# Attention and feed-forward on one core: the first batch's queries and keys in two transfers, and a given order of decoding, mix and scores

## The chip, the cores and the metric

The kernel runs on one core of one Trainium2 chip. A core has five engines with instruction streams of their own: TensorE (PE; its weight loads are listed apart as PEld), VectorE (DVE), ScalarE (ACT), GpSimd (POOL) and SyncE (SP), whose queue issues the transfers between device memory and the on-chip memory. The metric is the device time of one execution in microseconds (us); less is better.

## The reference

The inputs are 8 batches of 8 heads with 512 local and 32 global tokens of 64 numbers. A local query attends to the 32 global keys and to the local keys at most 32 positions away; a global query attends to all 544 keys. The result, as 576 tokens of 512 numbers, goes through a feed-forward part that mixes each token with the one ahead of it:

```python
    s_g = scale * np.matmul(q_g, k_all.transpose(0, 1, 3, 2))
    out_g = np.matmul(sm(s_g), v_all)
    mask = np.abs(pos[:, None] - pos[None, :]) <= window
    s_ll = np.where(mask, s_ll, -1000000000.0)
    a_l = sm(np.concatenate([s_lg, s_ll], axis=-1))
    out_l = np.matmul(a_l, np.concatenate([v_g, v_l], axis=2))
...
    xk = mu_k * x + (1.0 - mu_k) * x_prev
    xr = mu_r * x + (1.0 - mu_r) * x_prev
    k = np.maximum(xk @ w_k, 0.0)
    v = k * k @ w_v
    r = 1.0 / (1.0 + np.exp(-(xr @ w_r)))
    return (r * v).astype(np.float32)
```

The queries, keys and values are float32 and the weights w_k (512 x 1024), w_r (512 x 512) and w_v (1024 x 512) are float64.

## The kernel before, in words

**Attention.** Two heads lie side by side on the 128 partitions as one unit, so that a batch has four units, and two units make a pair. For each unit one array `qk` holds on 128 rows the 64 columns of global queries, the 512 of local queries and the 896 of windows of keys (1536 columns, 768 KB), and another, `v`, the values. `scores` (the multiplications are recorded at L359 in `Run.matmul`) multiplies queries of 64 tokens with a window of 160 keys on PE. DVE adds the mask and takes the greatest of each row (L331), ACT takes exponentials and their sums (L337, eight for a call), DVE makes the inverse of the sums (L294, L295) and POOL multiplies by it (L347, four operations, into `Pt` and `Pgl`). `scores_global` does the like for the global queries of a pair (L411 and L415 on DVE, L419 on ACT, L421 on POOL, result `Pg`). `transposes` and `transposes_of_g` turn the result on PE (L384, L393), and DVE and ACT copy it to `PT` and `PTg` (L386, L394); `transposes_global` does this for `Pg` (L434, copies to `PG` at L435). `weighted` multiplies by the values and copies the tokens to `xT` (L488 on ACT) and to `xg_all` (L483 and L485 on DVE).

**Batch 0.** Its two pairs are cut into halves of 256 tokens. This gives four groups of scores, here R0 (pair 0, first half), R1 (pair 1, first half), R2 (pair 0, second half) and R3 (pair 1, second half), and two global ones. From batch 1 on a generator interleaves the attention of the next batch with the feed-forward part of the one before.

**Feed-forward.** `Tokens` stands for 256 tokens. `Tokens.mix` computes for two blocks of 128 numbers at a time (`c0` is 0 or 2) the difference to the token ahead (L521) and, for the keys (`xk`) and then the gate (`xr`), the mixed value `xfull` (L525). ACT rounds it to a first part (L529: `xkh`, `xrh`), and POOL makes the rest (L530: `xkl`, `xrl`). Block 0 comes from pair 0 and block 2 from pair 1. `keys_and_gate` makes `xk @ w_k` with three products for each pair of blocks (L496, L497, L498, in `products`: first part by first part of the weight, rest by first part, first part by rest), then `relu` on ACT (L541), its square on POOL (L543) and as first part and rest on ACT (L546) and DVE (L547). `gates` and `values` do the same with w_r and w_v.

**Weights.** The float64 weights are read as 64-bit integers in 20 chunks of 128 x 512 (512 KB): 0 to 7 of w_k, 8 to 11 of w_r, 12 to 19 of w_v. `decode` makes float32 of them: ACT scales the high word (L192), DVE shifts and joins the bits in three operations (L193, L196, L199), ACT rounds to a first part (L205) and POOL subtracts (L206), so that `wk_h` and `wk_l` (or `wr`, `wv`) sum to the weight. The first four chunks have a buffer each. The others share a ring of three: the load of chunk n+3 (`load_chunk`, L177) waits for POOL's L206 of chunk n. `weights` is a generator; each `next(decoding)` decodes one chunk and asks for the next load.

**Order.** Each engine runs its instructions in one fixed order. The tile scheduler makes it at build time, from the program's order of statements, a model of times and explicit constraints: `tc.issue_after(i)` keeps what is recorded within it behind instruction `i`. Transfers are issued by SP in the order in which the loads are written (L282 for `raw_qk`, L287 for `raw_v`, L177 for chunks, L854 for `mu_k` and `mu_r`). The start of batch 0 is written out by hand at the end of the main function. Eight masks, one for each half and each of four places, are made by POOL with 16 `affine_select` (L126, L130).

## Time and profile before

| what | value |
|---|---|
| median of three runs | 693.78 us (692.35, 693.78, 924.29) |
| the profiled execution | 695.92 us |
| its span, from first to last instruction | 694.0 us |
| mean granted clock of TensorE | 0.98 |
| moved by DMA | 123.37 MB, 178 GB/s over the span |
| queue issues of `w_k` chunks, median to landing | 9.7 us |
| queue issues of `w_r` chunks, median to landing | 4.0 us |

The run of 924.29 us is far from the two others and is left out of every reading. The profiled execution is one more execution; it spends 1.9 us outside its span. In a timeline a row gives the start, the duration, the engine, line and operation, output and inputs, and in brackets the idle time ahead of it with what ended it. Line numbers are those of the kernel before.

### The profile page before, as it was taken

To read this page: it belongs to the slowest core of one execution; us is meant where nothing else is said; L and a number is where in the kernel's file an instruction comes from. 1 tells how busy PE (TensorE), PEld (TensorE's weight loads), DVE (VectorE), ACT (ScalarE), POOL (GpSimd) and SP (SyncE) were. 2 spreads that over 40 slices of the span, in tenths; PEclk is the share of its full clock that TensorE was granted. 3 is DMA by queue.
4 is the path that set the end of the run, shared out by engine and by line. 5 is a ranking of instruction groups with operands and counts; after the bars stand their busy time and mean duration, and the time that the engine had idled before them with its cause. 6 is when DMAs were issued, how large, how long until landed. Compare 5 with 4: busy or idle time off the path is not lost.

```text
span 694.0 us, 18613 instructions
## 1 busy us (share of the span) xinstructions
PE 659.8 (95%) x7472; PEld 621.6 (90%) x7472; DVE 428.0 (62%) x1217; ACT 387.0 (56%) x1058; POOL 360.1 (52%) x363
## 2 busy tenths in 40 slices
PE   4879999999998899999999999999999999999997
PEld 2658788999897899999999999999999999999996
DVE  5767987356647575555685656646675656377531
ACT  5756886356355456566557473757366644453530
POOL 5656596137967434564428353655348342642810
PEclk9659999999999999999999999999999999999999
DMA  9732535153736641452909083644728081535666
GB/s 343 295 97 104 212 124 196 47 184 122 245 137 239 213 175 75 157 209 105 350 7 338 26 318 138 221 145 180 277 76 291 2 323 43 197 119 170 204 198 207
DMA packets 43542, 123.37 MB, mean 178 GB/s; under 512 B 4032, under 2 KB 20928, under 8 KB 43456
## 3 DMA queue, kind: packets, MB, share of 16 engines
q1 hardware_dynamic: 43456, 122.18, 49.4%
q8 instruction: 59, 0.97, 0.6%
q14 instruction: 27, 0.22, 0.1%
HBM read 104.86 MB, written 17.30 MB: 176 GB/s over the span
## 4 chain that ended last, share of the span: by engine, by line
PE 63%; DVE 12%; POOL 9%; DMA 8%; ACT 5%; issue 3%; SPq 0%; POOLq 0%; ACTq 0%; DVEq 0%
PE ps_m L652 14%; PE ps_m L497 11%; PE ps_m L496 11%; PE ps_m L498 11%; PE ps_s L363 8%; DMA a<-scratch 6%; PE ps_t L384 3%; ACT Pt L337 2%; DVE xfull L525 2%; DVE diff L521 2%; DMA w<-w_r 2%; DVE Pt L331 2%; PE ps_s L365 1%; POOL Pt L347 1%; DVE kkl L547 1%
## 5 line engine op out<-in xcount | busy, mean ns | idle before, releaser
L496 PE MATMUL ps_m<-xkh,wk_h 128*128 128x256 f32 x544 | 154.9, 285 | 2.2 <-ACT xkh L529 1.0
L497 PE MATMUL ps_m<-xkl,wk_h 128*128 128x256 f32 x544 | 153.5, 282 | 0.5 <-POOL xkl L530 0.4
L498 PE MATMUL ps_m<-xkh,wk_l 128*128 128x256 f32 x544 | 153.2, 282 | 0.0
L652 PE MATMUL ps_m<-bh,a 128*128 128x256 f32 x736 | 137.8, 282 | 2.8 <-DMA a<-scratch 2.8
L337 ACT ACTIVATE Pt<-Pt,m 128x160 f32<-128x160 f32 x256 | 106.5, 418 | 29.0 <-DVE m L331 27.7
L652 PEld LDWEIGHTS ps_m<-bh,a 128*128 128x128 f32 x736 | 115.0, 188 | 6.1 <-DMA a<-scratch 3.1
L347 POOL TENSOR_TENSOR Pt<-Pt,ssum 128x512 f32<-128x512 f32 x64 | 67.9, 1061 | 82.2 <-DVE ssum L295 34.9
L496 PEld LDWEIGHTS ps_m<-xkh,wk_h 128*128 128x128 f32 x544 | 103.1, 190 | 4.1 <-ACT xkh L529 1.2
L497 PEld LDWEIGHTS ps_m<-xkl,wk_h 128*128 128x128 f32 x544 | 103.0, 189 | 1.6 <-POOL xkl L530 1.0
L498 PEld LDWEIGHTS ps_m<-xkh,wk_l 128*128 128x128 f32 x544 | 103.0, 189 | 0.3 <-issue 0.2
L652 PE MATMUL ps_m<-bl,a 128*128 128x256 f32 x368 | 102.6, 279 | 0.0
L530 POOL TENSOR_TENSOR xkl<-xfull,xkh 128x512 fp32r<-128x512 f32 x34 | 46.7, 1374 | 89.8 <-ACT xkh L529 84.8
L564 DVE TENSOR_TENSOR B<-ps_m,relu 128x512 f32<-128x512 f32 x52 | 35.9, 690 | 72.3 <-ACT relu L562 72.3
L562 ACT ACTIVATE relu<-ps_m 128x512 f32<-128x512 f32 x52 | 31.1, 597 | 83.8 <-PE ps_m L498 81.6
L496 PE MATMUL ps_m<-xrh,wr_h 128*128 128x256 f32 x272 | 77.2, 284 | 0.4 <-ACT relu L541 0.4
L497 PE MATMUL ps_m<-xrl,wr_h 128*128 128x256 f32 x272 | 76.3, 281 | 0.0
L498 PE MATMUL ps_m<-xrh,wr_l 128*128 128x256 f32 x272 | 76.1, 280 | 0.0
L331 DVE CUSTOM_DVE_ANT_0 Pt<-ps_s,masks 128x160 f32<-128x160 f32 x256 | 65.6, 317 | 7.4 <-PE ps_s L363 7.3
L652 PEld LDWEIGHTS ps_m<-bl,a 128*128 128x128 f32 x368 | 69.2, 188 | 0.0
L599 POOL TENSOR_TENSOR gate<-sum,gate 128x512 f32<-128x512 f32 x18 | 26.9, 1493 | 58.9 <-DVE sum L698 39.2
L205 ACT CAST bh<-B 128x512 fp32r<-128x512 f32 x76 | 45.9, 619 | 17.3 <-PE ps_m L652 10.8
L496 PEld LDWEIGHTS ps_m<-xrh,wr_h 128*128 128x128 f32 x272 | 51.5, 189 | 1.1 <-ACT relu L541 0.5
(138 smaller groups left out, 1586.1 us busy)
## 6 DMA issues: line engine op xcount, KB each, us to landing
a<-scratch SPq DMA_DIRECT2D x92, 512.0 KB, 6.2
raw_qk<-qk SPq DMA_DIRECT2D x32, 768.0 KB, 5.7
raw_v<-v SPq DMA_DIRECT2D x32, 640.0 KB, 6.4
out_l<-gate SPq DMA_DIRECT2D x32, 256.0 KB, 4.8
w<-w_k SPq DMA_DIRECT2D x8, 512.0 KB, 9.7
w<-w_v SPq DMA_DIRECT2D x8, 512.0 KB, 4.2
w<-w_r SPq DMA_DIRECT2D x4, 512.0 KB, 4.0
scratch<-wv_h SPq DMA_DIRECT2D x8, 256.0 KB, 2.7
```

Source lines behind the costliest of these rows:

```text
L205: nc.scalar.copy(hi, val)
L331: read = nc.vector.tensor_tensor_reduce(out=Pt[:, i], in0=place(e, t, h), in1=masks[:, e, slots[t][1]], op0=ALU.add, op1=ALU.min, scale=-s ...
L337: nc.scalar.activation(Pt[:, i], Pt[:, i], AF.Exp, bias=low_x[:, i:i + 1], scale=-1.0, accum_out=ssum[:, i:i + 1],)
L347: nc.gpsimd.tensor_mul(out, Pt[:, each, at:at + n], rinv.unsqueeze(2).to_broadcast([P, 4, n]))
L363: self.last = nc.tensor.matmul(*a, **kw)
L496: nc.tensor.matmul(out, w_h[:, i, cols], x_h(i), start=(i == 0), stop=False)
L497: nc.tensor.matmul(out, w_h[:, i, cols], x_l(i), start=False, stop=False)
L498: nc.tensor.matmul(out, w_l[:, i, cols], x_h(i), start=False, stop=(i == n - 1))
L530: nc.gpsimd.tensor_sub(lo[:, both], xf, hi[:, both].bitcast(F32))
L562: nc.scalar.activation(rk, kp, AF.Relu)
L564: nc.vector.tensor_mul(k2[f0 // HC][f0 % HC // 2], kp, rk)
L652: nc.tensor.matmul(out[:, j], w, x[:, i % 2], start=fresh and (i, j, n) == (0, 0, 0), stop=(i, n) == (HC - 1, 2), skip_group_check=True,)
```

## The change

It has five parts, all in the start of batch 0.

1. The columns of `qk` are put as global queries, first 256 local queries, keys, last 256 local queries. For batch 0 a unit is loaded in two transfers, of 832 columns (these hold the global queries, the first local queries and the keys of the first half) and of 704. The four first parts are issued ahead of everything else; the chunks come behind the second parts and values. For other batches it is one transfer as before, and `q(i)` finds a block of queries in the new order.
2. Four of the eight masks, which are equal to others, are copied by DVE, and the 16 selects become 8.
3. `mix` takes which mix to make (`of`) and for which blocks (`c0s`). For the first 256 tokens of batch 0 the mix for the keys of block 0, then of block 2, then the mix for the gate are recorded apart, and for the second 256 tokens the keys and the gate apart. The difference (L521) is computed in each call, so there are eight more of them in all.
4. `queued_after` puts what is recorded in it behind given instructions. With it, chunk 0 stands behind the copies of R0's transposes, chunk 1 behind those of R1, chunks 2 and 3 behind the first mix for the keys, R2's scores behind the second one and the values of the first halves, and chunks 4 and 5 and R3's scores behind the mix for the gate. Chunks 2 and 3 use the four-bank pool of PSUM instead of the two-bank one.
5. `weighted` returns its last matmul and copy, so that these can be waited for.

```diff
+    @contextmanager
+    def queued_after(*before):
+
+        with ExitStack() as stack:
+            for i in before:
+                stack.enter_context(tc.issue_after(i.ins))
+            yield
...
     def load_qk(s, pool=rawp, tag=""):
-        s.qk = pool.tile([P, K0 + SK], F32, tag="qk" + tag, name="raw_qk")
-        nc.sync.dma_start(out=s.qk, in_=qk[s.b, s.c])
-        s.q, s.k = s.qk[:, QG:K0], s.qk[:, K0:]
+
+        if s.b > 0:
+            cols = slice(None)
+        elif s.qk is None:
+            cols = slice(FIRST_PART)
+        else:
+            cols = slice(FIRST_PART, None)
+        if s.qk is None:
+            s.qk = pool.tile([P, QG + SL + SK], F32, tag="qk" + tag, name="raw_qk")
+            s.k = s.qk[:, K0:K0 + SK]
+        nc.sync.dma_start(out=s.qk[:, cols], in_=qk[s.b, s.c][:, cols])
...
-    load_qk(heads_0[0])
+    load_first(load_qk, range(NC))
+    load_first(load_qk, (0, 1))
+    load_first(load_v, (0, 1))
     load_chunk()
-    load_qk(heads_0[1])
+    load_first(load_qk, (2, 3))
     load_chunk()
...
     for sb, mu in ((mu_k_sb, mu_k), (mu_r_sb, mu_r)):
         nc.sync.dma_start(out=sb, in_=mu)
-    for _ in range(3):
+    load_first(load_v, (2, 3))
+    for _ in range(5):
         load_chunk()
-    R, Pg = [], []
-    for pair, bank in zip(pairs_0, "os"):
-        R.append(by_halves(pair, 0))
-        Pg.append(scores_global(pair, bank))
+    R = [by_halves(pair, 0) for pair in pairs_0]
+    Pg = scores_global(pairs_0[0], "o")
+    with queued_after(all_transposes(R[0])):
+        next_Pg = scores_global(pairs_0[1], "s")
+    with queued_after(*R[0].copies[1:]):
         next(decoding)
-    for i, pair in enumerate(pairs_0):
-        all_transposes(R[i])
-        PG, final, _ = transposes_global(Pg[i])
-        with tc.issue_after(final.ins):
-            weighted(pair, xTs_0[i], PG, (0,), "m")
+    PG, final, _ = transposes_global(Pg)
+    all_transposes(R[1])
+    with queued_after(*R[1].copies[1:]):
         next(decoding)
-        if i == 0:
-            R.append(by_halves(pair, 1))
+    with queued_after(final):
+        weighted(pairs_0[0], xTs_0[0], PG, (0,), "m")
+    PG, final, _ = transposes_global(next_Pg)
+    first[0].mix("k", (0,))
+    with queued_after(*first[0].mix_ends):
+        for _ in range(2):
+            next(decoding)
+    with queued_after(final):
+        values_made, _ = weighted(pairs_0[1], xTs_0[1], PG, (0,), "m")
+    first[0].mix("k", (2,))
+    with queued_after(values_made, *first[0].mix_ends):
+        R.append(by_halves(pairs_0[0], 1))
+    first[0].mix("r")
...
-    first[0].mix()
     next(keys[0])
     next(keys[0])
-    next(decoding)
-    next(decoding)
-    R.append(by_halves(pairs_0[1], 1))
+    with queued_after(*first[0].mix_ends):
+        next(decoding)
+        next(decoding)
+    with queued_after(values_made, *first[0].mix_ends):
+        R.append(by_halves(pairs_0[1], 1))
...
+        first[1].mix("k")
         for _ in keys[0]:
             next(decoding)
             yield
-        first[1].mix()
+        first[1].mix("r")
```

The lines of the changed kernel have other numbers: L282 becomes L313 (`raw_qk`), L287 L317 (`raw_v`), L177 L186 (chunks), L192 L201 (scaling), L205 and L206 L214 and L215 (rounding and split), L488 L518 (`xT`), L435 L465 (`PG`), L529 and L530 L563 and L564, L347 L377, L543 L581.

The loads on SP at the very start, before:

```order
L282 DMA raw_qk<-qk 128x1536
L177 DMA w_190<-w_k 128x512
L282 DMA raw_qk<-qk 128x1536
L177 DMA w_194<-w_k 128x512
L282 DMA raw_qk<-qk 128x1536 x2
L287 DMA raw_v<-v 128x1280 x2
L177 DMA w_204<-w_k 128x512
L177 DMA w_206<-w_k 128x512
L287 DMA raw_v<-v 128x1280 x2
```

and of the change:

```order
L313 DMA raw_qk<-qk 128x832 x4
L313 DMA raw_qk<-qk 128x704 x2
L317 DMA raw_v<-v 128x1280 x2
L186 DMA w_182<-w_k 128x512
L313 DMA raw_qk<-qk 128x704 x2
L186 DMA w_186<-w_k 128x512
```

The first chunk was the second transfer; it now stands behind eight others. (The names with `w_` are chunks; each number is one buffer.)

ACT around the copies of the first tokens (`xT`), before:

```order
L192 ACTIVATE w_216<-w_216 128x512
L192 ACTIVATE w_218<-w_218 128x512
L488 COPY xT<-ps_t 128x2x2x64
L205 CAST wk_h<-w_204 128x512
L205 CAST wk_h<-w_214 128x512
L205 CAST wk_h<-w_216 128x512
L488 COPY xT<-ps_t 128x2x2x64
L386 COPY PT<-ps_t 128x512
L529 CAST xkh<-xfull 128x512
```

and of the change:

```order
L201 ACTIVATE w_186<-w_186 128x512
L518 COPY xT<-ps_t 128x2x2x64
L201 ACTIVATE w_202<-w_202 128x512
L214 CAST wk_h<-w_186 128x512
L518 COPY xT<-ps_t 128x2x2x64
L465 COPY PG<-ps_t 128x512
L465 COPY PG<-ps_t 128x128
L563 CAST xkh<-xfull 128x512
```

The scaling of `w_202`, chunk 6 and the last that is issued at the start, now stands between the two copies of the first pair's tokens, and the first `xkh` follows the copies of `PG`.

POOL's splits of the chunks of w_k and the first of w_r, from the first `xkl` on, before:

```order
L530 TENSOR_TENSOR xkl<-xfull,xkh 128x512
L530 TENSOR_TENSOR xrl<-xfull,xrh 128x512
L206 TENSOR_TENSOR wk_l<-w_218,wk_h 128x512
...
L206 TENSOR_TENSOR wk_l<-w_290,wk_h 128x512
L206 TENSOR_TENSOR wk_l<-w_206,wk_h 128x512
L530 TENSOR_TENSOR xkl<-xfull,xkh 128x512
L530 TENSOR_TENSOR xrl<-xfull,xrh 128x512
L543 TENSOR_TENSOR k_643<-relu 128x512
L543 TENSOR_TENSOR k_676<-relu 128x512
L206 TENSOR_TENSOR wr_l<-w_362,wr_h 128x512
```

and of the change, from the second `xkl` on:

```order
L564 TENSOR_TENSOR xkl<-xfull,xkh 128x512
...
L564 TENSOR_TENSOR xrl<-xfull,xrh 128x512 x2
L581 TENSOR_TENSOR k_633<-relu 128x512
L215 TENSOR_TENSOR wk_l<-w_198,wk_h 128x512
L581 TENSOR_TENSOR k_666<-relu 128x512
L215 TENSOR_TENSOR wk_l<-w_200,wk_h 128x512
...
L215 TENSOR_TENSOR wk_l<-w_202,wk_h 128x512
L215 TENSOR_TENSOR wk_l<-w_355,wk_h 128x512
...
L215 TENSOR_TENSOR wr_l<-w_392,wr_h 128x512
```

In each place that is left out stand the four norms of one group of scores (L347, now L377). The splits of chunks 4 to 7 (`w_198`, `w_200`, `w_202`, `w_355`) stood ahead of the second `xkl` and now stand behind it, behind the first squares and between norms.

More of the change, by code (lines that the diff above doesn't have):

```diff
@@ L1 @@
-from contextlib import ExitStack
+from contextlib import ExitStack, contextmanager
 from itertools import chain
@@ L119, in local_global_attention_then_rwkv_ffn, with in_window @@
     nc.gpsimd.memset(masks, 0.0)
[L120 to L133 removed]
+    def in_window(e, p, a):
+        return masks[a * BL:(a + 1) * BL, e, p, SG * e:SG * e + W]
+    same = {}
+    for e, p in ((1, 0), (0, 0), (0, 1), (1, 1)):
+        for a, i in enumerate(PAIRS[e][p]):
+            m = in_window(e, p, a)
+            ahead = FIRST[i] - BL * i + SG
+            if (a, ahead) in same:
+                nc.vector.tensor_copy(m, same[a, ahead])
+                continue
+            same[a, ahead] = m
+            nc.gpsimd.affine_select(
+                out=m, in_=m, pattern=[[1, W]], base=ahead, channel_multiplier=-1,
+                compare_op=ALU.is_ge, fill=NEG,
+            )
+            nc.gpsimd.affine_select(
+                out=m, in_=m, pattern=[[-1, W]], base=2 * SG - ahead, channel_multiplier=1,
+                compare_op=ALU.is_ge, fill=NEG,
+            )
     low = const.tile([P, 3 * W], BF16, name="low")
@@ L491, in weighted @@
                 )
+        return run.last, copied
     def products(out, w_h, w_l, cols, x_h, x_l, n):
@@ L510, in wide, with mix @@
             return mixp.tile([P, NC, TOK], dtype, tag="mix", name=name)
-        def mix(self):
+        def mix(self, of="kr", c0s=range(0, NC, 2)):
             got = []
-            for mu, nm in ((mu_k_sb, "k"), (mu_r_sb, "r")):
-                got.append((mu, self.wide(f"x{nm}h", F32R), self.wide(f"x{nm}l", F32R)))
-            for c0 in range(0, NC, 2):
+            for x in of:
+                if x not in self.mixed:
+                    self.mixed[x] = tuple(self.wide(f"x{x}{part}", F32R) for part in "hl")
+                got.append(({"k": mu_k_sb, "r": mu_r_sb}[x], *self.mixed[x]))
+            for c0 in c0s:
                 both = slice(c0, c0 + 2)
@@ L528, in mix @@
                         )
-                    nc.scalar.copy(hi[:, both], xf)
+                    cut = nc.scalar.copy(hi[:, both], xf)
                     nc.gpsimd.tensor_sub(lo[:, both], xf, hi[:, both].bitcast(F32))
-            (_, self.xk_h, self.xk_l), (_, self.xr_h, self.xr_l) = got
+                    if x == "k":
+                        self.xk_h, self.xk_l = hi, lo
+                    else:
+                        self.xr_h, self.xr_l = hi, lo
+            self.mix_ends = mixed, cut
         def keys_and_gate(self):
@@ L830, in local_global_attention_then_rwkv_ffn @@
     keys = [t.keys_and_gate() for t in first]
-    decoding = weights(range(EARLY), wk_h, wk_l, "m")
+    decoding = chain(weights(range(2), wk_h, wk_l, "m"), weights(range(2, EARLY), wk_h, wk_l))
     def by_halves(pair, p):
```

45 lines of the change are left out of this document (17 added, 28 removed).

## The prediction

> **What bounds the kernel now.** I read the page first, then the busy time by stretches, then the timelines of the engines around the places that the diff touches. The page says whose kernel it is:
>
> ```profile
> span 694.0 us, 18613 instructions
> PE 659.8 (95%) x7472; PEld 621.6 (90%) x7472; DVE 428.0 (62%) x1217; ACT 387.0 (56%) x1058; POOL 360.1 (52%) x363
> ```
>
> PE is busy 95% of the span, so only the 34.2 us in which it is not can be won, besides time in which it works slowly. The stretches (busy us of PE, PEld, DVE, ACT, POOL; then the granted clock and the DMA share) say where both lie:
>
> ```profile
> 0.00:56.00 56.00, 37.86 (x397) 27.19 (x397) 38.16 (x139) 34.24 (x105) 33.00 (x55) 0.76 0.63 235
> 56.00:112.80 56.80, 54.41 (x625) 48.73 (x626) 48.85 (x137) 45.24 (x126) 39.90 (x38) 1.00 0.49 169
> 112.80:117.80 5.00, 4.20 (x39) 3.96 (x37) 2.80 (x4) 2.93 (x8) 5.00 (x7) 1.00 0.50 203
> 117.80:694.00 576.20, 563.32 (x6416) 541.73 (x6416) 338.17 (x938) 304.62 (x821) 282.17 (x266) 1.00 0.49 173
> ```
>
> The first 56 us hold 18.1 us of idle PE and a clock of 0.76; the 576 us behind 117.8 hold 12.9 us of idle PE. The change touches the first part alone: from the values of batch 0 on, PE's instructions stand in the same order before and after, and so, in kind, do those of the other engines. So the whole effect is how much earlier or later PE passes one place, the product with the last piece of w_v, which ends the start:
>
> ```profile
> 4.93 1.34 PE L359 MATMUL ps_s<-raw_qk 64*64 64x160 f32 x16 [4.93 <-DMA raw_qk<-qk]
> 55.95 0.39 PE L497 MATMUL ps_m<-xkl,wk_h 128*128 128x256 f32 x1 [0.45 <-POOL xkl L530]
> 117.78 0.38 PE L498 MATMUL ps_m<-kkh,wv_l 128*128 128x256 f32 x1 [0.80 <-POOL wv_l L206]
> ```
>
> The three rows (start, duration, what ended the idle time) are the start's three marks: the first keys land at 4.93, the mixed tokens of the second pair reach PE at 55.95, the last decoded weight reaches it at 117.78. Between the second and third mark PE waits little, yet it is not alone: every chunk has to pass through ACT, DVE, ACT and POOL, and the next load into the ring of three waits for POOL:
>
> ```profile
> SPq L177 <- POOL wk_l L206: 23.7, 4, 10.9
> SPq L177 <- POOL wv_l L206: 23.1, 5, 12.1
> SPq L177 <- POOL wr_l L206: 8.1, 3, 4.2
> ```
>
> (Total us, times, longest.) These are waits of the load queue up to 120 us; 12 of the chunks' loads leave only when an older chunk is through. So there are two chains: tokens to PE up to 56, and chunks to PE up to 117.8. An earlier end needs both.
>
> **The change, part by part. The first loads.** Now the first scores wait for transfers and masks thus:
>
> ```profile
> 5.80 1.65 POOL L130 TENSOR_SCALAR_AFFINE_SELECT masks<-masks 64x128 bf16<-64x128 bf16 x5
> 6.78 0.67 ACT L192 ACTIVATE w<-w 128x512 f32<-128x512 f32 x1 [4.76 <-DMA w<-w_k]
> 9.57 0.33 DVE L331 CUSTOM_DVE_ANT_0 Pt<-ps_s,masks 128x160 f32<-128x160 f32 x1
> 10.80 0.41 ACT L337 ACTIVATE Pt<-Pt,m 128x160 f32<-128x160 f32 x1
> 18.90 0.41 ACT L337 ACTIVATE Pt<-Pt,m 128x160 f32<-128x160 f32 x1
> ```
>
> Masks are complete at 7.45, chunk 0 is decoded ahead of the scores on DVE, and the exponentials of the first halves (R0 and R1) end at 19.3. After the change 0.43 MB instead of 0.79 MB must land for a unit. Rates, from the 5-us stretches:
>
> ```profile
> 10.00:15.00 5.00, 2.71 (x37) 1.48 (x35) 4.59 (x23) 5.00 (x20) 1.44 (x2) 0.97 1.02 424
> 25.00:30.00 5.00, 3.82 (x77) 3.50 (x76) 3.73 (x9) 4.92 (x17) 1.70 (x3) 0.83 0.97 394
> 30.00:35.00 5.00, 5.00 (x40) 3.79 (x37) 4.96 (x9) 2.02 (x4) 5.00 (x5) 0.50 0.07 22
> 45.00:50.00 5.00, 5.00 (x59) 4.66 (x58) 1.91 (x7) 1.46 (x3) 4.79 (x6) 0.50 0.33 108
> ```
>
> The last number is GB/s: the transfers fill the DMA engines up to 30 us at some 0.41 MB/us. The part left out is 0.36 MB, 0.85 us, so the first unit lands at 4.93 − 0.85 = 4.1 and each further first part 1.05 later. Eight selects become four copies on DVE; eight times 0.33 (1.65 for five) leaves the masks ready at about 4.8. Scores of R0 then start near 5.8 instead of 9.57, since no decoding stands ahead of them, and 8 exponentials of 0.41 run from 6.2 to 9.5. R1 needs the second pair's parts (8.3 and 9.2 with the load order) and ends its exponentials near 15.5: 3.8 us ahead of 19.3. The four extra transfers cost SP about 0.45 us each at the issue; the queue is behind the DMA engines' rate anyway, so nothing on the path.
>
> **The tokens.** From there I followed the new order by durations of rows: transposes, values of the first pair 21.4 to 24.5 on PE, copy of its tokens by ACT at 23.3. Next in ACT's order stands the scaling of chunk 6, the last of the 9.44 MB issued at the start. At 0.407 MB/us from 3.1 on, that lands at 26.3; so a new wait of 2.6 us on ACT, with the second token copy, two PG copies and the first xkh behind it, and DVE's mix and PE's next values behind those. It is of the kind that this row shows before, where token copies stand behind the scaling of a chunk that lands late:
>
> ```profile
> 50.18 0.69 ACT L192 ACTIVATE w<-w 128x512 f32<-128x512 f32 x1 [2.83 <-DMA w<-w_r]
> 50.77 0.62 ACT L488 COPY xT<-ps_t 128x256 f32<-128x256 f32 x2
> 51.15 0.89 DVE L521 TENSOR_TENSOR diff<-xT 128x256 f32<-128x256 f32 x1 [4.24 <-ACT xT L488]
> 54.61 1.28 POOL L530 TENSOR_TENSOR xkl<-xfull,xkh 128x512 fp32r<-128x512 f32 x1 [2.85 <-ACT xkh L529]
> ```
>
> With it, the first xkh comes at 29.0, the second pair's values at 28.6 to 33.8 (half clock), the second xkh at 37.6 and its xkl at 39.5 in place of 55.9. That is 16.4 us earlier; 1.8 us of PE work which stood ahead of the mark (scores of R3, transposes of R2) now stands behind it, so PE's lead is 14.6 us. The extra differences on DVE, eight with 4 of them here, at this price, and the multiplications of the gate's mix, which no longer stand in the way, are in that chain:
>
> ```profile
> 35.43 0.41 DVE L521 TENSOR_TENSOR diff<-xT 128x256 f32<-128x256 f32 x1
> ```
>
> **The chunks.** At 39.5 only chunks 0 to 3 are decoded; before, the last of eight was split at 51.8:
>
> ```profile
> 49.19 2.57 POOL L206 TENSOR_TENSOR wk_l<-w,wk_h 128x512 fp32r<-128x512 f32 x2
> ```
>
> Chunks 4 and 5 come behind the scores of R2 and the mix for the gate, 6 and 7 behind R3. The marks of the last gate chunk (11) are now:
>
> ```profile
> 64.96 0.39 SPq L177 DMA_DIRECT2D w<-w_r  x1
> 69.66 0.69 ACT L192 ACTIVATE w<-w 128x512 f32<-128x512 f32 x1 [1.59 <-DMA w<-w_r]
> 70.38 0.69 DVE L193 TENSOR_SCALAR ps_s<-w 128x512 int32<-128x512 int32 x1 [1.40 <-ACT w L192]
> 73.38 1.44 POOL L206 TENSOR_TENSOR wr_l<-w,wr_h 128x512 fp32r<-128x512 f32 x1 [1.05 <-ACT wr_h L205]
> 75.64 0.39 PE L498 MATMUL ps_m<-xrh,wr_l 128*128 128x256 f32 x1
> ```
>
> The load leaves at 64.96, DVE is on it at 70.38 and PE uses it at 75.64. A load of this kind takes 4.0 us to landing when it goes alone:
>
> ```profile
> w<-w_r SPq DMA_DIRECT2D x4, 512.0 KB, 4.0
> ```
>
> In the new order, by pitches of 0.6 for an operation of ACT or DVE on 128x512, 0.25 for a score, 0.41 for an exponential, 1.3 for a split and some 3 for four norms: the first relu is at 43.0 and chunk 4 is scaled behind it (43.6), its split ends at 50.4; chunk 7's load leaves then and lands at 54.3. Chunk 5's split at 52.8 frees chunk 8, scaled at 60.0 behind six exponentials of batch 1; chunks 6 and 7 are split by 58.6 and 59.9. Chunk 8's split, behind another pair of norms, ends at 69.0, and chunk 11 loads from 69.0 to 73.0: DVE on it at 73.7, **3.3 us later** than before. PE's 14.6 us are gone in waits for chunks 4 to 11. From chunk 11 on, the rows that carry the rest are
>
> ```profile
> 75.60:113.50 37.90, 35.51 (x408) 31.38 (x404) 34.43 (x109) 31.68 (x90) 26.72 (x26) 1.00 0.53 184
> 99.67 1.79 DVE L547 TENSOR_TENSOR kkl<-k,kkh 128x512 fp32r<-128x512 f32 x1 [0.33 <-POOL k L543]
> 103.34 0.61 DVE L415 CUSTOM_DVE_ANT_0 Pg<-ps_t,low,mg 128x384 f32<-128x384 f32 x1
> 112.08 0.69 DVE L199 SCALAR_TENSOR_TENSOR w<-w,ps_s 128x512 int32<-128x512 int32 x1
> 112.96 1.06 POOL L347 TENSOR_TENSOR Pt<-Pt,ssum 128x512 f32<-128x512 f32 x1
> 115.71 0.58 POOL L347 TENSOR_TENSOR Pgl<-Pt,ssum 128x128 f32<-128x128 f32 x1
> 116.25 1.48 POOL L206 TENSOR_TENSOR wv_l<-w,wv_h 128x512 fp32r<-128x512 f32 x1
> ```
>
> DVE is busy 34.4 of 37.9 us there: its order is the bound, not PE. Between chunk 11 and the last chunk it has in the new order one kkl (1.3 as a mean of such rows), one global score (0.8) and three small copies (0.4) fewer and two differences (0.8) more: **−1.7**. Of its 3.5 idle us I credit **−0.5**, since PE's results now wait for it. On POOL the four norms (112.96 to 116.29) stand between the last two splits; in the new order they stand ahead of both, where they start some 2.5 us before DVE ends. The last split then comes 3.2 us behind DVE's end instead of 5.0: **−1.8**. Sum: 3.3 − 1.7 − 0.5 − 1.8 = −0.7.
>
> A second way to the same end: of DVE's 38.2 us up to 56, the new order has at 39.5 left for later four chunks (12 operations, 7.4), R3's scores (2.0), the gate's mix (1.6) and a transpose copy (0.6), so some 26 to 27 are done. Of 87 us up to the last decoding, plus 3.3 for eight differences, less 1.7 put behind it, 62.5 remain. At the share of the second stretch (48.85 of 56.80, 86%) this ends at 39.5 + 72.7 = 112.2, against 112.77; with POOL's −1.8, −2.4. I take the middle of the two ways, **−1.5**. At the 91% of the row above it would end at 108.3 and the sum be −6.3; without any idle time at 102: these bound the gain, and no case of a gain beyond 12.6 is left unless DVE does less.
>
> **A rule that speaks against it.** PE's waits for chunks 4 to 11 could cost clock. The two 5-us rows above, at 30 and 45, show PE busy for all of 5.00 us at a granted 0.50, and the second stretch shows 1.00. The Trainium skill, page "TensorE: Matmul & The Clock Gate", section "Part 1: The HAM clock gate", says that TensorE falls to half rate after an idle window of about 3.4 us and comes back only after a busy one; by that rule each long wait would cost an estimated 1.7 us behind it. The trace agrees in that rows of both 0.50 and 1.00 exist, but not that a busy stretch suffices. Without the rule: a wait for chunk 11 longer than any PE has now would leave some 5 us at 0.50 as in those rows, a loss of 2.5 us each. As long as it comes ahead of 77, PE waits for chunk 11 anyway and it is hidden; behind that it is not.
>
> **The rivals.** (a) *The decoding keeps up*: chunk 6 lands earlier than 26.3 or the norms of R2 and R3 are cheaper to pass, chunk 11 is not late, DVE runs at 91%. The gain is 4.0 (the sum without its +3.3) to 8; 686 to 690. For it speaks that ACT and POOL have idle time in all stretches; against it, that all five late loads hang on splits queued behind scores and relus. (b) *The chunks set the end, later*: the place is chunk 8's split, which frees chunk 11's load. Each us that it ends after 64.9 goes to the end, since DVE has nothing to catch up with; it decides from 3.5 us on, where the credits on DVE and POOL (4.0) are spent. With DVE's credits gone (+2.2) the sum is +1.5, and with chunk 8 behind four more norms (3.3) it is +4.8: 695 to 699, slower than before. For it: chunk 8 is scaled behind exponentials of the next batch. (c) *The clock*: two waits behind 77 at 2.5 us, 5.0 with the −1.5: about 697. (d) *The lead is kept*: the decoding is not in the way at all, −14.6, 679. DVE's 62.5 us left speak against it. That the first loads do not come earlier can be left out: a first part has 54% of the bytes.
>
> **How the numbers follow.** The forecast has 0.45, (a) 0.26, (b) 0.21, (c) 0.04, (d) 0.04. The profiled execution took 695.9 us (694.0 of it in the span), 2.1 above the median of 693.8. 695.9 − 1.5 = 694.4 for such an execution, **692.3** against the median. Range: down to 685, most of (a), up to 700, nearly all of (b) and (c). Two per cent, what a measurement of this kernel can tell, are 13.9 us: faster by that only with (d) and no trouble, 0.05 with the tail of (a); slower by that 0.03; within it 0.92.
>
> **What would show it.** Right: first score on DVE near 5.8 and exponentials of R1 done by 15.5; the scaling of chunk 6 waiting for its load with token copies behind; the second xkl near 39.5; PE idle by some 12 us or more between 40 and 78, waiting for wk and wr pieces; chunk 11's load leaving at 67 to 71; DVE 85 to 91% busy from 40 on; the last wv_l at 115 to 118. Wrong: PE still 5 us or more ahead at the gate's fourth chunk (before 70.6), which is (a) or (d); the last wv_l behind 119, which is (b) if chunk 11 was late, (c) if the clock shows below 1.00 behind 77.

## The result, and the profile after

The change is slower: 703.25 us as the median of four runs (700.53 to 705.41). Its ratio to the kernel before on the same chip is 1.0107 with a 95% interval of 1.0068 to 1.0146, some 7.4 us. The kernel before has a median of 693.78 us in three runs of that comparison; a fourth, of 924.29 us, is left out here (with it the median would be 695.14). The medians alone would give 9.5 us, so 7.4 rests on a second set as well: four runs of the change against 20 of the kernel before gave 703.14 us and 1.0106 (1.0081 to 1.0131). The prediction of 692.3, range 685 to 700, was wrong; of its rivals (b), the chunks that set the end, is nearest. The profiled execution took 700.53 us, at the low end of its runs.

The first mark is the busy time up to the last split of w_v and behind it (columns as in the prediction), of the change:

```profile
0.00:126.20 126.20, 101.25 (x1055) 82.79 (x1055) 97.57 (x290) 82.62 (x236) 75.70 (x89) 0.91 0.52 188
126.20:698.80 572.60, 563.80 (x6417) 542.78 (x6417) 337.98 (x940) 305.00 (x822) 281.46 (x267) 1.00 0.49 174
```

and of the kernel before:

```profile
0.00:117.70 117.70, 96.44 (x1056) 79.86 (x1056) 89.81 (x279) 82.34 (x237) 77.80 (x98) 0.88 0.56 202
```

The start ends 8.5 us later. DVE is busy for 97.57 us in it instead of 89.81, 7.8 more, and idle for 28.6 instead of 27.9. Behind it PE has the same work (563.8 and 563.3 us); how much it waits there differs from one execution to the next: the stretch took 572.6 us here, 576.3 before, and 576.4 in a second profile of the change, in which the last split ended at 126.3. So for this kernel the end of the start is the steadier measure of the two, and its 8.5 us answer to the 7.4 of the ratio. Between different kernels it does not decide alone, as the table of experiments will show.

Where DVE's time went is in one group, first before and then in the change (busy us, mean ns, idle ahead of them):

```profile
L521 DVE TENSOR_TENSOR diff<-xT 128x256 f32<-128x256 f32 x10 | 5.1, 529 | 5.3 <-ACT xT L488 5.2
```

```profile
L555 DVE TENSOR_TENSOR diff<-xT 128x256 f32<-128x256 f32 x18 | 12.6, 728 | 1.7 <-ACT xT L518 1.6
```

With eight more differences the group is 7.5 us longer, 0.94 for each where the prediction took 0.41; all 18 take 0.73 on average, the ten before 0.53 (two of each count are batch 1's). DVE and POOL beside each other show why. DVE in the change, around the mixes of the second pair:

```profile
37.55 1.53 DVE L559 SCALAR_TENSOR_TENSOR xfull<-diff,mu_k_sb,xT 128x256 f32<-128x256 f32 x1
38.99 1.85 DVE L555 TENSOR_TENSOR diff<-xT 128x256 f32<-128x256 f32 x2
40.77 0.47 DVE L559 SCALAR_TENSOR_TENSOR xfull<-diff,mu_k_sb,xT 128x256 f32<-128x256 f32 x1
...
43.91 0.75 DVE L555 TENSOR_TENSOR diff<-xT 128x256 f32<-128x256 f32 x2
```

and POOL at that time:

```profile
37.49 2.73 POOL L215 TENSOR_TENSOR wk_l<-w,wk_h 128x512 fp32r<-128x512 f32 x2 [3.72 <-ACT wk_h L214]
41.97 1.28 POOL L564 TENSOR_TENSOR xkl<-xfull,xkh 128x512 fp32r<-128x512 f32 x1 [1.74 <-ACT xkh L563]
```

Two differences take 0.75 us while POOL is idle (43.25 to 45.94) and 1.85 where it splits chunks until 40.22 (from 37.49); an `xfull` takes 0.47 and 1.53.

The marks of the tokens and of the chunks in the change, on PE:

```profile
4.14 1.35 PE L389 MATMUL ps_s<-raw_qk 64*64 64x160 f32 x16 [4.14 <-DMA raw_qk<-qk]
...
43.30 0.58 PE L528 MATMUL ps_m<-xkl,wk_h 128*128 128x256 f32 x1 [0.69 <-POOL xkl L564]
...
83.41 0.58 PE L529 MATMUL ps_m<-xrh,wr_l 128*128 128x256 f32 x1 [0.76 <-POOL wr_l L215]
...
126.26 0.38 PE L529 MATMUL ps_m<-kkh,wv_l 128*128 128x256 f32 x1 [0.27 <-POOL wv_l L215]
```

PE is 12.65 us ahead at the second mark (55.95 before), 7.8 behind at the fourth product of w_r (75.64) and 8.5 behind at the last of w_v (117.78). The steps between stand on ACT:

```profile
7.48 0.43 ACT L367 ACTIVATE Pt<-Pt,m 128x160 f32<-128x160 f32 x1 [5.47 <-DVE m L361]
...
16.93 0.43 ACT L367 ACTIVATE Pt<-Pt,m 128x160 f32<-128x160 f32 x1
...
28.40 0.65 ACT L201 ACTIVATE w<-w 128x512 f32<-128x512 f32 x1 [3.61 <-DMA w<-w_k]
28.96 0.63 ACT L214 CAST wk_h<-w 128x512 fp32r<-128x512 f32 x1
29.49 0.37 ACT L518 COPY xT<-ps_t 128x256 f32<-128x256 f32 x1
...
47.39 0.60 ACT L579 ACTIVATE relu<-ps_m 128x512 f32<-128x512 f32 x1 [1.17 <-POOL Pgl L377]
47.88 1.26 ACT L201 ACTIVATE w<-w 128x512 f32<-128x512 f32 x2
...
76.62 0.68 ACT L201 ACTIVATE w<-w 128x512 f32<-128x512 f32 x1 [2.33 <-DMA w<-w_r]
```

and on DVE and POOL:

```profile
7.11 0.33 DVE L361 CUSTOM_DVE_ANT_0 Pt<-ps_s,masks 128x160 f32<-128x160 f32 x1 [2.29 <-PE ps_s L389]
...
78.99 0.69 DVE L202 TENSOR_SCALAR ps_s<-w 128x512 int32<-128x512 int32 x1
...
122.14 0.69 DVE L208 SCALAR_TENSOR_TENSOR w<-w,ps_s 128x512 int32<-128x512 int32 x1
```

```profile
53.48 1.31 POOL L215 TENSOR_TENSOR wk_l<-w,wk_h 128x512 fp32r<-128x512 f32 x1 [1.29 <-ACT wk_h L214]
...
71.80 1.31 POOL L215 TENSOR_TENSOR wr_l<-w,wr_h 128x512 fp32r<-128x512 f32 x1
...
123.22 2.99 POOL L215 TENSOR_TENSOR wv_l<-w,wv_h 128x512 fp32r<-128x512 f32 x2
```

The wait for chunk 6 ahead of the token copy is there (3.61 us); the first relu and the scaling of chunk 4 behind it are at 47 to 48; chunk 4's split ends at 54.8, chunk 8's at 73.1, and DVE begins chunk 11 at 78.99, behind squares, two differences and a global score.

### The profile page after: what moved, and what is told of

Same layout as the page of the kernel before. It is cut to its first block, busy times and chain, and to the rows that moved or that the text cites. A ratio compares the mean times of both kernels' runs of the same rounds, so it can differ in the third digit from the quotient of the medians.

```text
span 698.8 us, 18610 instructions
## 1 busy us (share of the span) xinstructions
PE 665.0 (95%) x7472; PEld 625.6 (90%) x7472; DVE 435.5 (62%) x1229; ACT 387.6 (55%) x1058; POOL 357.2 (51%) x355
## 4 chain that ended last, share of the span: by engine, by line
PE 65%; DVE 10%; POOL 5%; ACT 2%; DMA 2%; issue 2%; POOLq 0%; ACTq 0%
PE ps_m L690 17%; PE ps_m L527 11%; PE ps_m L528 11%; PE ps_m L529 11%; PE ps_s L393 9%; PE ps_t L414 3%; DMA a<-scratch 2%; DVE xfull L559 2%; DVE Pt L361 2%; DVE diff L555 2%; PE ps_s L395 2%; DVE B L671 1%; POOL a L262 1%; DVE T L671 1%; DVE B L602 1%
## 5 line engine op out<-in xcount | busy, mean ns | idle before, releaser
L527 PE MATMUL ps_m<-xkh,wk_h 128*128 128x256 f32 x544 | 156.9, 289 | 6.0 <-ACT relu L579 3.1
L528 PE MATMUL ps_m<-xkl,wk_h 128*128 128x256 f32 x544 | 155.6, 286 | 0.9 <-POOL xkl L564 0.9
L529 PE MATMUL ps_m<-xkh,wk_l 128*128 128x256 f32 x544 | 154.8, 285 | 1.0 <-POOL wk_l L215 1.0
L377 POOL TENSOR_TENSOR Pt<-Pt,ssum 128x512 f32<-128x512 f32 x64 | 67.6, 1056 | 96.9 <-DVE ssum L325 47.0
L527 PEld LDWEIGHTS ps_m<-xkh,wk_h 128*128 128x128 f32 x544 | 105.1, 194 | 8.6 <-ACT relu L579 3.6
L528 PEld LDWEIGHTS ps_m<-xkl,wk_h 128*128 128x128 f32 x544 | 105.1, 193 | 2.7 <-POOL xkl L564 1.4
L529 PEld LDWEIGHTS ps_m<-xkh,wk_l 128*128 128x128 f32 x544 | 104.8, 193 | 1.6 <-POOL wk_l L215 1.6
L564 POOL TENSOR_TENSOR xkl<-xfull,xkh 128x512 fp32r<-128x512 f32 x34 | 46.7, 1373 | 86.3 <-ACT xkh L563 81.4
L527 PE MATMUL ps_m<-xrh,wr_h 128*128 128x256 f32 x272 | 78.4, 288 | 1.5 <-ACT relu L579 1.4
L529 PE MATMUL ps_m<-xrh,wr_l 128*128 128x256 f32 x272 | 77.3, 285 | 1.0 <-POOL wr_l L215 1.0
L555 DVE TENSOR_TENSOR diff<-xT 128x256 f32<-128x256 f32 x72 | 49.0, 718 | 13.9 <-ACT xT L518 13.6
L214 ACT CAST bh<-B 128x512 fp32r<-128x512 f32 x76 | 45.9, 619 | 17.3 <-PE ps_m L690 10.9
```

Of the source, the lines that this page charges most:

```text
L214: nc.scalar.copy(hi, val)
L377: nc.gpsimd.tensor_mul(out, Pt[:, each, at:at + n], rinv.unsqueeze(2).to_broadcast([P, 4, n]))
L527: nc.tensor.matmul(out, w_h[:, i, cols], x_h(i), start=(i == 0), stop=False)
L528: nc.tensor.matmul(out, w_h[:, i, cols], x_l(i), start=False, stop=False)
L529: nc.tensor.matmul(out, w_l[:, i, cols], x_h(i), start=False, stop=(i == n - 1))
L555: nc.vector.tensor_sub(self.shape(diff[:, j]), self.cur(c0 + j), self.prev(c0 + j))
```

## The experiments

The theories: A, the chunks are decoded too late in the given order; B, the extra differences cost it, as work on DVE; C, the first loads push the chunks back; later D, the loss is in where pieces of the order stand, and E, late chunks 4 and 5 and differences share it. Each kernel was compared with the kernel before on the same chip; us are 695 times the ratio less one. "Chunk 11" is the end of the split of chunk 11, the last of w_r, and "last split" that of w_v, each in one profile.

| kernel | median us | ratio to before, 95% interval | against before, us | chunk 11 | last split |
|---|---|---|---|---|---|
| the kernel before | | 1 | 0 | 74.8 | 117.7 |
| the change | 703.25 | 1.0107 (1.0068 to 1.0146) | +7.4 | 83.4 | 126.2 |
| e18, the change once more | 703.14 | 1.0106 (1.0081 to 1.0131) | +7.4 | 83.6 | 126.3 |
| e1, loads and masks, order of before | 703.38 | 1.0108 (1.0077 to 1.0139) | +7.5 | 81.3 | 130.5 |
| e2, given order, loads of before | 700.99 | 1.0089 (1.0059 to 1.0118) | +6.2 | 88.9 | 124.3 |
| e3, both mixes together | 694.75 | 0.9992 (0.9970 to 1.0014) | −0.6 | 77.5 | 121.7 |
| e5, two more buffers for chunks | 701.87 | 1.0078 (1.0043 to 1.0114) | +5.4 | 82.6 | 122.7 |
| e6, before with the copied masks | 695.79 | 1.0011 (0.9991 to 1.0032) | +0.8 | 75.0 | 118.9 |
| e7, first differences kept | 704.60 | 1.0147 (1.0130 to 1.0165) | +10.2 | 91.8 | 127.8 |
| e8, before with eight more differences | 699.01 | 1.0064 (1.0040 to 1.0089) | +4.4 | 74.6 | 122.1 |
| e10, second tokens' mixes together | 700.63 | 1.0085 (1.0068 to 1.0101) | +5.9 | 82.5 | 125.1 |
| e11, chunks 4 and 5 ahead | 705.80 | 1.0137 (1.0113 to 1.0161) | +9.5 | 86.6 | 130.0 |
| e12, e3 and two more buffers | 699.43 | 1.0041 (1.0021 to 1.0061) | +2.8 | 77.7 | 122.0 |
| e13, before and two more buffers | 696.00 | 1.0004 (0.9984 to 1.0024) | +0.3 | 74.7 | 119.5 |
| e14, e11 and e10 in one | 705.16 | 1.0123 (1.0098 to 1.0148) | +8.5 | 89.2 | 133.6 |
| e15, extra differences left out | 699.46 | 1.0049 (1.0032 to 1.0066) | +3.4 | 82.7 | 123.3 |
| e16, before, differences on POOL | 698.92 | 1.0037 (1.0018 to 1.0056) | +2.6 | 80.7 | 125.1 |
| e17, extra differences on POOL | 701.55 | 1.0091 (1.0064 to 1.0118) | +6.3 | 85.6 | 124.0 |
| e19, e3 with differences twice | 702.38 | 1.0080 (1.0052 to 1.0108) | +5.6 | 78.7 | 125.6 |
| e20, e3 with the loads of before | 699.77 | 1.0048 (1.0024 to 1.0071) | +3.3 | 78.4 | 121.3 |

**e1**: the new layout, parts and masks, with the statements of before behind the loads (`R, Pg = [], []` down to R3's scores, and `first[1].mix()` in its old place).

> The new layout, the loads in two transfers and the copied masks alone; the order of decoding, mix and scores is left to the scheduler as it was before. Theory A (the chunks of weights are decoded too late in the given order): the last gate chunk is back on DVE near 70 instead of 79, and the time is that of before or 1 to 4 us less, 690 to 695. Theory B (eight more differences and slower DVE operations cost it): the same, 690 to 695. Theory C (the first loads push the chunks back): the first-issued chunks still land late, ACT waits for one by 3 us or more, and 5 us or more of the loss stay, 698 to 703.

None of these as a whole: 7.5 us are lost without the given order and without an extra difference. Of theory C the remaining loss comes true, but not the wait (the longest of ACT for a chunk of w_k is 2.6 us), and the time is just above its range. DVE is idle for 37 us up to the last split, 9 more than in the kernel before; the scheduler, left alone with the other loads, places things worse. So this run does not speak for the given order being harmful.

**e2**: the change with the load order and whole transfers of before.

```diff
-        if s.b > 0:
+        if s.b >= 0:
             cols = slice(None)
```

> The given order of the change, with the loads of before: whole queries and keys, chunks between them. Theory A: the last gate chunk is as late as in the change, on DVE at 76 to 80, and the time stays 5 to 9 us above before, 699 to 703. Theory B: the same, 699 to 703. Theory C: the wait of ACT for the chunk ahead of the token copy is gone and the time is that of before within 3 us, 692 to 697.

6.2 us stay: theory C is out as the main cause in the given order.

**e3**: keys and gate mixed together.

```diff
-    first[0].mix("k", (0,))
+    first[0].mix("kr", (0,))
...
-    first[0].mix("k", (2,))
+    first[0].mix("kr", (2,))
...
-    first[0].mix("r")
...
-        first[1].mix("k")
...
-        first[1].mix("r")
+        first[1].mix()
```

> The change with the mix for keys and gate made together from one difference, so with eight differences fewer. Theory A: one to three us better than the change at most, 699 to 702, the last gate chunk on DVE at 76 or later. Theory B: DVE is 4 us or more ahead at that chunk, and half or more of the loss is gone, 694 to 698. Theory C: as the change, 701 to 704.

The whole loss is gone. That is theory B's side, though two things differ: eight differences, and the place of the gate's mix. Theory A's forecast misses, yet its mechanism is not out: the constraints on the chunks are the same in words, but "behind the mix" now means an earlier place, and the chunks come earlier. Chunk 4's split ends at 49.8 instead of 54.8, and DVE begins chunk 11 at 72.60 instead of 78.99:

```profile
72.60 0.69 DVE L202 TENSOR_SCALAR ps_s<-w 128x512 int32<-128x512 int32 x1 [0.16 <-ACT w L201]
```

The last split is nevertheless 4.0 us later than in the kernel before (121.7), while the time is the same.

**e5** gives chunks 4 and 5 buffers of their own in `first_units` and loads seven chunks at the start instead of five.

> The change with buffers of their own for chunks 4 and 5 (in space that is free until the values' weights), so that chunks 7 and 8 are loaded at the start and 9 to 11 wait for the splits of chunks 6 to 8. Theory A, if the ring of three is the link: the last gate chunk is on DVE 3 us or more earlier, by 76, and the time 2 to 6 us below the change, 697 to 701; if DVE's own order is the link, the loads leave earlier and nothing ends earlier, 702 to 704. Theories B and C: 702 to 704.

About 2 us better than the change, with overlapping intervals. DVE begins chunk 11 at 74.2, as theory A asked, but other work stands between its three operations, and its split ends at 82.6 instead of 83.4. So the ring alone is not the main link; the order of other work moved here too. **e13** does the same to the kernel before and keeps POOL's order:

> The kernel before with buffers of their own for chunks 4 and 5; the order on POOL is the same. If the ring of three and its loads (6.0 us of waits of ACT for w_r) set the end of the start in the kernel before: 688 to 692. If they are only beside it, since DVE has the same work: 693 to 697.

Nothing: the second xkl reaches PE at 53.84 instead of 55.95, and the 2 us are not seen at the end. **e12** adds the buffers to e3:

> The change with keys and gate mixed together everywhere (694.75 in its own run) and buffers of their own for chunks 4 and 5, so that chunks 7 and 8 are loaded at the start. If the wait of ACT for chunk 7's and 8's loads still sets that kernel's end: 689 to 693, better than before. If DVE's order alone does: 693 to 697.

It is slower than e3 by 3.4 us, in neither range; with the loads the scheduler moved other work.

**e6** has only the masks of the change:

> The kernel before with four of the eight masks copied by DVE, and nothing else. All theories: 693 to 697, as before; more than 3 us above it would say that the scheduler's own order, moved by a small edit, makes differences of the size that is to be explained.

As before. The masks are no cause.

**e8** is the kernel before with each difference computed once more ahead of the gate's `xfull`:

```diff
+                    if again and mu is mu_r_sb:
+                        diff = self.two(tmpp, "diff")
+                        for j in range(2):
+                            nc.vector.tensor_sub(self.shape(diff[:, j]), self.cur(c0 + j), self.prev(c0 + j))
```

> The kernel before, with each of batch 0's eight differences computed once more ahead of the mix for the gate; nothing else is changed. Theory B (DVE's work sets the end of the start, and eight differences of 0.9 us beside a busy POOL are most of the loss): 4 to 8 us above before, 699 to 703. Theory D (the loss is where the pieces of the order stand, and 3.3 us of differences at 0.41 hide in DVE's 28 us of idle time): within 2 us of before, 693 to 697.

4.4 us, theory B's range. Its stretch up to the last split:

```profile
0.00:122.10 122.10, 97.75 (x1060) 80.76 (x1061) 95.38 (x287) 82.48 (x238) 78.31 (x98) 0.89 0.53 195
```

DVE is busy 5.6 us longer and idle 1.2 less (26.7), which gives the 4.4 by which the last split is late. Chunk 11's split still ends at 74.6 (74.8 before): all of it is lost behind chunk 11, where the second tokens' differences stand.

**e7** keeps the first tokens' differences in `first_units` for the gate's mix and mixes the second ones together:

> The order of the change, but the differences of the first 256 tokens are kept in a buffer of their own for the mix for the gate, and the second 256 tokens are mixed for keys and gate together: no difference is computed twice. Theory B: as before within 3 us, 692 to 698. Theory D: as the change, 700 to 704, since the first tokens' mix for the gate stands where it stood in the change.

Theory D's side, and worse than the change: no difference is computed twice, and 10.2 us are lost. DVE is idle for 33.5 us in it.

**e10** is the change with `first[1].mix()` in the place of `first[1].mix("k")`:

> The change with the second 256 tokens mixed for keys and gate together: four differences fewer, and all up to chunk 11 as in the change. Theory B: half of the way back, 697 to 701. Theory D, if the place is ahead of chunk 11: as the change, 701 to 705.

1.5 us back by the ratios, with overlapping intervals. The median lies at the upper end of theory B's range, but the gain is less than its half.

**e11** moves one constraint of the change:

```diff
     first[0].mix("k", (2,))
+    second_mix = first[0].mix_ends
+    decoding = weights(range(EARLY, NK), wk_h, wk_l)
+    with queued_after(*second_mix):
+        next(decoding)
+        next(decoding)
-    with queued_after(values_made, *first[0].mix_ends):
+    with queued_after(values_made, *second_mix):
         R.append(by_halves(pairs_0[0], 1))
```

> The change with one constraint moved: chunks 4 and 5 stand behind the second mix for the keys, ahead of the second half's scores, the mix for the gate and the first relu, instead of behind these. All eight extra differences stay. Theory E (two causes: chunk 4, split at 54.8 in the change and at 35.2 before, starts the chain of the chunks too late, which is worth 3 to 5 us, and the extra differences, worth 4 us): chunk 4's split ends by 50, chunk 11's by 80, and the time is 697 to 700.5. If the place of chunks 4 and 5 is not in the chain: 702 to 705 as the change.

Chunk 4's split ends at 49.6, as asked, and the rest is later: POOL waits 4.76 us for a relu, and chunk 6's split stands behind it and four norms.

```profile
48.33 1.31 POOL L215 TENSOR_TENSOR wk_l<-w,wk_h 128x512 fp32r<-128x512 f32 x1 [0.78 <-ACT wk_h L214]
...
57.20 1.04 POOL L581 TENSOR_TENSOR k<-relu 128x512 f32<-128x512 f32 x1 [4.76 <-ACT relu L579]
...
62.55 1.30 POOL L215 TENSOR_TENSOR wk_l<-w,wk_h 128x512 fp32r<-128x512 f32 x1 [1.12 <-ACT wk_h L214]
```

Theory E's first half falls: the place of chunk 4 alone does not carry the chain. **e14** has four differences fewer:

> The kernel with chunks 4 and 5 ahead, and the second 256 tokens mixed for keys and gate together (four differences fewer). Theory E: 2 to 3 us below the one with chunks 4 and 5 ahead, 694 to 698; without it: as that one within 1.

It is 1.0 us below e11, within their intervals: theory E misses here as well.

**e15** leaves the gate's differences out (`self.cur(c0 + j) if of == "r" else ...` as input of `xfull`):

> The change, with the gate's differences of batch 0 left out (the mix for the gate takes the token itself instead of its difference, so that part of the gate is not the reference's); eight operations fewer on DVE, the scheduler's order nearly that of the change. If the extra differences are the cause: 4 to 8 us below the change, 695 to 699. If the order costs as much without them: 702 to 705.

```profile
0.00:123.30 123.30, 102.68 (x1061) 83.77 (x1061) 92.19 (x283) 82.31 (x236) 74.56 (x89) 0.90 0.54 193
```

4.0 us of the 7.4 are gone, at the edge of the first range, with DVE busy 5.4 us less than in the change and idle 2.5 more. Up to chunk 11 hardly anything is won: DVE begins it at 78.35, 0.6 us earlier.

```profile
78.35 0.69 DVE L202 TENSOR_SCALAR ps_s<-w 128x512 int32<-128x512 int32 x1
```

**e17** makes them on POOL instead:

> The change with the eight differences of the gate's mix made by POOL. If the cause is DVE's work: 2 to 6 us below the change, 697 to 701, unless POOL's splits get late by it. If it is the order: 702 to 706.

Between the two: DVE's load falls, POOL's rises. **e16** moves the eight differences of the kernel before to POOL:

> The kernel before with the eight differences of batch 0 made by POOL, so with 4 to 5 us less work on DVE up to the last split. If DVE's work sets the end of the start: 2 to 4 us below before, 691 to 693. If POOL's order, with differences ahead of splits, is as near the bound: 694 to 699.

It is in the second range. DVE is busy 87.5 us, 2.3 less, but idle 37.5; it waits for POOL's differences (7.2 us), and 2.6 us are lost. Less work on DVE is not enough where the work moves to an engine with a queue of its own. **e18** is the change itself:

> The change once more, word for word. All theories: 701 to 705; its last split between 124 and 129, or else the end of the start is no measure of the run.

Both hold: 703.14 us, and the last split at 126.3.

**e19** computes the differences twice in e3:

> Keys and gate mixed together in the given order, but each of the eight differences computed a second time for the gate. If differences cost 4 us wherever they stand, and the place of the gate's mix the other 4: 697.5 to 700.5. If the extra differences are all of the loss in this order: 701 to 704.

The median is in the second range; against before, which ran 1 to 2 us slower in that comparison, it is +5.6, some 6 us above e3. So in this order the differences cost more than the 4.4 of e8, and nearly all of the loss. As in e8, most of it is lost behind chunk 11, which DVE begins when it does in e3:

```profile
72.58 0.69 DVE L202 TENSOR_SCALAR ps_s<-w 128x512 int32<-128x512 int32 x1 [3.66 <-ACT w L201]
```

**e20** gives e3 the loads of before:

> Keys and gate mixed together in the given order, with the loads of the kernel before (whole units, chunks between them). If the first loads in two parts cost 2 us, as their removal from the change suggests: 691 to 694, better than both kernels. If they gain what they were sized at, 3.8 us ahead at the first exponentials: 696 to 699. If neither reaches the end: 694 to 696.

3.9 us worse than e3, with a median just above the second range. But the start does not end later: the last split is at 121.3, in e3 at 121.7. So the 3.9 us lie behind the last split in these profiles, and that they are the 3.8 us which the first loads were sized at is not shown. No kernel beat the one before; e3 equals it.

## Why the prediction was wrong, step by step

**The bound** was read rightly for the change: the last split moved by 8.5 us for 7.4 in the time. That the whole effect is when PE passes that place is too strong: the last split is 4.0 us late in e3 for no loss, 12.8 in e1 for 7.5, and 15.9 in e14 for 8.5. What is made up behind it stays open.

**The first loads** land as predicted (4.14 for 4.1), but DVE's scores start at 7.11 and the exponentials of R1 end at 17.4 instead of 15.5, since the new order puts R0's inverse and the global scores between them.

**The tokens**: the new wait of ACT is where it was said, 3.6 us for 2.6, and chunk 6 is scaled at 28.4 instead of 26.3. The second xkl reaches PE at 43.3 for 39.5 forecast: `xfull` and differences run beside chunk splits at two to three times their price. The `xfull` at 37.55 and the two differences behind it take 3.4 us, where 0.47 and 0.41 each would give 1.3. How much of the 3.8 us each of these carries is not shown.

**The chunks**: this term failed first. The relu ahead of chunk 4 came at 47.4 instead of 43.0, and each link behind it, from chunk 4's split (54.8 for 50.4) to chunk 8's (73.1 for 69.0), 4 us late with it. Chunk 11 is scaled by 77.3, but the second tokens' differences, 2.42 us beside POOL's splits, and half a global score keep DVE from it for 1.7 us more. The term was sized at +3.3 and measured +8.6 (78.99 against 70.38).

**From chunk 11 on**: −1.7 and −0.5 were credited on DVE; it took 43.8 us from there to the end of the last decoding (122.83) against 42.4 before (112.77), +1.4. DVE's work fell by 0.8 us there (38.66 against 39.44), half of what was forecast, since six differences took 3.1 us where the four before took 1.6; its idle time grew by 2.2 us instead of falling by 0.5. The credit on POOL held: the last split ends 3.4 us behind DVE instead of 5.0, −1.6 for −1.8. The sum, 8.6 + 1.4 − 1.6 = 8.4, is the delay.

**The steps that failed** are thus two terms of the sum. Between the forecast of −0.7 and the 8.4 measured lie 9.1 us: 5.3 in the chunk term, 3.6 on DVE from chunk 11 on, 0.2 on POOL. Four kernels in the given order part the two things that the change did to the gate's mix, to make it apart from the keys' and to compute its differences again:

| the gate's mix | its own differences | against before, us | chunk 11 | last split |
|---|---|---|---|---|
| apart | made (the change) | +7.4 | 83.4 | 126.2 |
| apart | left out (e15) | +3.4 | 82.7 | 123.3 |
| beside the keys' | made (e19) | +5.6 | 78.7 | 125.6 |
| beside the keys' | none (e3) | −0.6 | 77.5 | 121.7 |

*The chunk term* goes with the place of the gate's mix, not with the differences. Chunk 11's split ends at 82.5 to 91.8 in all nine kernels of the given order with the first tokens' gate mix apart, and at 77.5 to 78.7 in the four with it beside the keys' (e3, e12, e19, e20); with or without the extra differences it moves by 0.6 to 1.2 us. So what the prediction mis-sized is the place "behind the scores of R2 and the mix for the gate": it gave that 3.3 us. Which link carries the lateness is not settled: neither other loads (e2), nor chunks 4 and 5 ahead (e11), nor kept differences (e7) bring chunk 11 back.

*The price of the differences* falls mostly behind chunk 11, in three pairs of kernels: 4.4 us in e8 against the kernel before, some 6 in e19 against e3, and 4.0 that leaving them out gives back in e15. e8, in which POOL's order is nearly that of before, is the cleanest; in e15 and e19 other work moved too. The prediction counted the differences, eight at 0.41, with no second end to the price, although a row quoted there has one of 0.89 at 51.15, and rows of DVE before,

```profile
32.66 1.41 DVE L525 SCALAR_TENSOR_TENSOR xfull<-diff,mu_k_sb,xT 128x256 f32<-128x256 f32 x1
33.99 1.51 DVE L525 SCALAR_TENSOR_TENSOR xfull<-diff,mu_r_sb,xT 128x256 f32<-128x256 f32 x1
```

stand beside POOL's

```profile
31.02 4.21 POOL L206 TENSOR_TENSOR wk_l<-w,wk_h 128x512 fp32r<-128x512 f32 x3
```

At 0.94 the eight are 7.5 us.

How the loss divides between the two is open. By the time, against e3, the place alone costs 4.0 us (e15), the differences alone 6.2 (e19), and both together 8.0 (the change), so the two overlap. By the last split the place is worth only 0.6 to 1.7 us and the differences 2.9 to 4.0, and e3 itself is 4.0 late, so the two measures do not agree on the shares. Each of these kernels also moved other work, and e1 and e7 show that such a shift alone is worth several us.

**The second way**, DVE's share, would have come nearer: up to the last split DVE was busy 76.3% before and 77.3% in the change. With the differences at 0.94, the masks' copies and an idle time that stays as it is, it would have said 8 us later. That is hindsight: the idle time did stay in the change (28.6 for 27.9), but in e1 and e7 it is 37.2 and 33.5. The rival (b) had the place, chunk 8's split, which ended at 73.1 instead of 64.5, but its price ended at +4.8.

**The clock** (c): its sign came, a granted clock below 1.00 behind 77.

```profile
80.00:85.00 5.00, 3.29 (x22) 2.64 (x21) 5.00 (x22) 3.50 (x12) 2.31 (x2) 0.81 0.80 288
100.00:105.00 5.00, 4.68 (x27) 4.68 (x28) 4.61 (x9) 4.50 (x12) 4.35 (x4) 0.66 0.27 99
```

It is not the main cause: chunk 11 is 8.6 us late at 78.99 already, ahead of both rows. In the second profile of the change (e18) the first of these dips is missing,

```profile
80.00:85.00 5.00, 3.28 (x28) 2.64 (x27) 5.00 (x21) 3.46 (x14) 2.33 (x2) 1.00 0.86 285
```

and the last split ends at the same time, 126.3 for 126.2; what the second dip costs was not measured. Up to there the clock is 0.91 in the change against 0.88 before.

## What to carry to other kernels

When an engine has idle time but is in order, price added work at its full duration beside its neighbours, and ask whether the idle time is yours to fill: DVE had 28 us of it before, and in e8 5.6 us of added work still moved the end by 4.4. Where an edit both adds work and moves it, build each half alone, as the four kernels above do. Take an operation's price from the rows where the neighbour engine is busy, not from the shortest row. A gain of 13 us at an inner mark says little as long as another chain, here the decoding, arrives last.

## What the runs showed of the hardware

DVE operations that read two inputs from SBUF, the main on-chip memory, can stretch beside POOL. Over the whole execution of the change, the 35 differences that ran while POOL was idle took 0.41 to 0.43 us, and the 11 that ran beside it for their whole length 0.41 to 1.55, with a median of 0.70. The 96 `xfull` with POOL idle took 0.47 to 0.49, and the 11 beside it 0.55 to 1.53, with a median of 1.51. Decoding operations, which have one input or read the other from PSUM, the memory of PE's results, kept their 0.68 to 0.69 us on average in all kernels. The Trainium skill, page "SBUF — State Buffer", section "Who interferes with whom", says that a DVE instruction with two SBUF inputs contends with a GpSimd instruction that reads SBUF. The rows of this case agree; no run here took POOL's work away to measure it apart.
